# The z1 matmuls of an attention and MLP kernel: operand in shared half-blocks, each row half with its own bank

## The chip, the cores and the metric

The kernel runs on one core of a Trainium2 chip. The metric is the time of one execution in microseconds (us), as the device measures it; it is given as the median of several runs.

## The reference, cut to what matters

One block with two branches that read the same normalised input: attention with 32 heads of 16, and a gated MLP in which z1, one half of the hidden layer, is a plain projection with a gelu.

```python
xn = _layernorm(x, axis=-1)                  # x: 1 x 2048 x 512
z  = _gelu(xn @ w_in)                        # w_in: 512 x 1792
z1 = z[..., :896]
z2 = _layernorm(z[..., 896:], axis=-1)
g  = einsum("ts,bsf->btf", w_sp, z2) + b_sp[None, :, None]   # w_sp: 2048 x 2048
out = x + attention(xn) + (z1 * g) @ w_out
```

All is float32. Where a product needs it, an operand is kept as a high and a low part, and three matmuls stand for one.

## The kernel before, in words

The program is written out instruction by instruction by a planner that runs when the kernel is built. It keeps a clock for each engine (`T`), hands work to TensorE (PE), ScalarE (ACT), VectorE (DVE) and GpSimd (POOL) in that order of time, and so fixes the order of every queue. On the chip only semaphores hold an instruction back; the planner's times are no longer looked at.

Attention sets the beat. PE goes through rounds: eight steps of values (`values`, L1471) in a burst, then eight scores (`scores`, L1363), seven to nine maxima for a later head pair (`maxima`, L1377), and between these the dense slots (`dense_slot`, L1428). The rows of `ORDER` say in which order; two rows alternate, one with nine maxima, one with seven. A dense slot is two matmuls at once, one on PE's upper 64 rows into one bank (`dps[0]`), one on the lower 64 rows into the other. Where PE would have to wait for a PSUM slot and no dense slot may run, the planner puts in a filler (L1442), a slot that multiplies by zero. A dense piece of work that ends more than eight slots into a round stops dense work until the next burst of values ("q", `hold`).

Dense work is a queue of stages: values' projection, q and k (`qk_rest`), `z2_all`, `z1_all`, `spatial` (w_sp times z2), `mlp_out`, `attn_out`.

z1 is computed as 7 blocks f of 128 features by 4 groups g of 512 rows of x, in 14 pairs: for each g the blocks (0, 1), (2, 3), (4, 5), and for odd g block 6 of g - 1 and g together. A pair is 24 slots, one round. The operands are `xnT[g, c]` for the four 128-row parts c of the contraction, and `w1[f]`, each a tile of 128 partitions x 2 parts x 512. Since a matmul has only 64 rows, each part c is split over the two row halves of PE: `both` (L415) first runs the upper half of the contraction of one block and the lower half of the other, then yields "s" and runs the two exchanged, so that each bank is finished by the row half that did not begin it. At an "s" `has_dense` (L1412) puts a `drain` on PE where the last dense slot isn't known to be over.

Transfers are issued by SyncE (SP) with `move`, in the planned order, on one queue. `ahead_of_time` (L356) writes the parts of the z1 weights to the scratch w1scr while the values' projection runs, and `fetch_parts` fetches them from row block NT - 3 of z2 on. `fetch_first` (L603) fetches the four blocks of g = 0 in the last row block of z2; `fetch_xnT` fetches the next group's in the rounds before it is wanted. Each is one DMA of 512 KB over 128 partitions. Tiles come from a ring of 18 (`room["big"]`) and, later, 8 more (`room["old"]`); `place` takes one, `leave` and `lease` give it back, and a "C" task waits until its condition on the rooms holds. `late1` and `kept` are numbers of tiles that weight fetches must leave free.

Names in what follows: dps, the two banks of dense work; wf, fetched weight parts (of w1 or w_sp); zs, the operand of `spatial`, whose pieces are moved by two DMAs of 64 partitions each; qst and kst, the stacked q and k, moved by DMAs of 48 partitions; qst<-mscr, the rows with the running maxima, which the scores need; xt, the operand of z2.

Of the kernel before, what the change touches and what calls it, by code (L numbers as in the profile page):

```python
# [16 lines left out]
P = 128  # L17
S = 2048
D = 512
# [61 lines left out]
LOAD = 5.0  # L81
LOADZ = 6.5
SETTLE = 4.0
HALF = 2.7
SLOT = 0.23
TURN = 0.2
# [6 lines left out]
def fused_block(ctx, tc, x, wqkv, wo, w_in, w_spT, b_sp, w_out, out):  # L93
# [57 lines left out]
    rscr = [[dr.tile([8, 512], F32, name=f"rscr{g}_{c}") for c in range(NG)] for g in range(4)]  # L151
    mscr = [dr.tile([4, 32, 32], F32, name=f"mscr{i}") for i in range(4)]
    wsscr = [dr.tile([P, 2, 512], F32, name=f"wsscr{s}") for s in range(KEPT)]
    w1scr = [dr.tile([P, 2, 512], F32, name=f"w1scr{f}") for f in range(NF)]
    bsplit = dr.tile([2, S], F32, name="bsplit")
    cscr = dr.tile([1, S], F32, name="cscr")
    bscr = [dr.tile([P, D], F32, name=f"bscr{t}") for t in range(NT)]
# [9 lines left out]
    def move(dst, src):  # L167
        nc.sync.dma_start(raw(dst), raw(src))

    def clock():  # L170
        return T["P"]
# [13 lines left out]
    def after(us, fn, *args):  # L185
        at(ends[0] + us, fn, *args)
# [169 lines left out]
    def ahead_of_time(k, a, scr, spare):  # L356

        out = {}
        yield from weight(out, k, a, spare)
        store(scr, out[k])  # L360
        after(2.5, leave, out, k)

    def fetch_parts(out, k, scr, spare):
        yield "C", lambda: clear() and room["big"] + room["old"] > 1 + spare[0]
# [53 lines left out]
        yield "s",  # L418
        yield from dense(n, y, x, (1, 0), False, True, w)

    def need(ok):
        while not ok():
            yield "w", 1.0

    held = [0]
    dfree = [0.0]
# [78 lines left out]
    def v_rest():  # L505

        for t in range(EARLY, NT, 2):
            k = None
            while dfree[0] > clock():
                if sum(f <= clock() for f in slotfree) > 1:  # L510
                    k = take("v", 2)
                    break
                yield "w", 0.05
            if t == VAHEAD:
                for f in range(NF):
                    owed[0] += 1
                    spawn(ahead_of_time(f, (f"w1_{f}", w_in[:, f * P:(f + 1) * P], D, ND), w1scr[f], AHEAD), 1)
                for s in range(KEPT):
                    owed[0] += 1
                    spawn(ahead_of_time(s, sp_weights(0, s), wsscr[s], AHEAD), 1)  # L520

            def ops(t):
                c128 = slice((t % 4) * P, (t % 4 + 1) * P)
                return lambda c: (xnT[t // 4, c][:, 0, c128], xnT[t // 4, c][:, 1, c128], wv[c][:, 0, :], wv[c][:, 1, :])
            for it in both(ND, ops(t), ops(t + 1)):
                if it[0] == "t" and k is not None:
                    it = "t", [[(2 + 2 * k + m[0], *m[1:]) for m in mms] for mms in it[1]]
                yield it
            if t in (2, 6):
# [68 lines left out]
            move(xt[:, :, c * P:(c + 1) * P], xscr[t // 4][c][:, :, (t % 4) * P:(t % 4 + 1) * P])  # L598

    late1 = [5]  # L600
    fetched = [False]

    def fetch_first():  # L603
        for c in range(ND):
            yield "C", lambda: room["big"] + room["old"] > 2
            xnT[0, c] = piece(f"xnT0_{c}_", place(xnT, (0, c)))
            move(xnT[0, c], xscr[0][c])
        fetched[0] = True
        late1[0] = 1

    def z2_all():
        yield from need(lambda: len(w2) == 2 * ND)
        for t in range(NT):
            xt = xts.pop(t)
            if t + 2 < NT:
                yield from need(lambda: room["big"] > 1)
                z2_load(t + 2)
            if t == NT - 6:
                calm[0] = False
            if t == NT - 3:  # L620
                for f in range(NF):
                    spawn(fetch_parts(w1, f, w1scr[f], late1), 1)
            if t == NT - 1:
                spawn(fetch_first(), 1)
            yield from need(lambda: room["big"] > 1)
            z = piece(f"z2_{t}").bitcast(F32).rearrange("p a b -> p (a b)")[:, :FH]
            ops = [lambda c, j=j: (xt[:, 0, c * P:(c + 1) * P], xt[:, 1, c * P:(c + 1) * P], w2[c, j][:, 0, :448], w2[c, j][:, 1, :448]) for j in range(2)]
            yield from both(ND, *ops, 448)
            lease("big", 1)
            yield "e", [z2_out(t, z, j) for j in range(2)]  # L630
            yield "q",
        for k in w2:
            leave(w2, k)

    def z1_out(f, g, bank):
        if bank == 0:
# [36 lines left out]
    kept = [3]  # L673

    def z1_all():
        yield from need(lambda: fetched[0])
        for g in range(NG):
            pairs = [((f, g), (f + 1, g)) for f in (0, 2, 4)]
            if g % 2:
                pairs.insert(0, ((6, g - 1), (6, g)))  # L680
            for n, pair in enumerate(pairs):
                if g == NG - 1 and n == 2:
                    load_b(0)
                    spawn(z_loader(), 2)
                    prepare(wsp, [((0, s), *sp_weights(0, s)) for s in range(KEPT, NT)], spare=kept)
                if (g, n) == FIRST:
                    for s in range(KEPT):
                        spawn(fetch_parts(wsp, (0, s), wsscr[s], kept), 1)
                if n == 2:
                    calm[0] = True  # L690
                if n == (2 if g % 2 else 1) and g + 1 < NG:
                    yield from need(lambda: room["big"] + room["old"] > 4)
                    fetch_xnT(g + 1, 1)
                yield from need(lambda: all(f in w1 for f, _ in pair))
                ops = [lambda c, f=f, h=h: (w1[f][:, 0, c * P:(c + 1) * P], w1[f][:, 1, c * P:(c + 1) * P], xnT[h, c][:, 0, :], xnT[h, c][:, 1, :]) for f, h in pair]
                yield from both(ND, *ops)
                if g == NG - 1:
                    for f in {f for f, _ in pair}:
                        leave(w1, f)
                if g % 2 and n == 0:  # L700
                    drop(g - 1)
                yield "e", [z1_out(f, h, i) for i, (f, h) in enumerate(pair)]
                yield "q",
            if g % 2:
                drop(g)

    def sp_weights(g, s):
        return f"wsp{g}_{s}", w_spT[s * P:(s + 1) * P, g * 512:(g + 1) * 512], 512
# [891 lines left out]
```

## Time and profile before

| | us |
|---|---|
| median of 3 runs | 1824.07 |
| lowest and highest | 1822.53, 1825.53 |
| the profiled execution | 1822.49 |
| its span, first to last instruction | 1820.6 |
| PE busy in the span | 1788.7 |
| DVE busy | 1442.1 |
| ACT busy | 1212.6 |
| POOL busy | 684.7 |

The times of the trace are microseconds from the start of the span. The z1 stage lies from 500 to 686 us of it: its first slot starts at 500.23, its last before the burst of values at 686. A busy share alone says little here: PE is nearly always busy, so it is read by the distance from one slot to the next and by the length of rounds.

### The profile page before, as it was taken

How to read it: one execution, taken by the hardware profiler on the slowest of the kernel's cores; microseconds unless marked ns; L12 is line 12 of the kernel's file. 1: busy time of each engine (PE TensorE's matmuls, PEld its weight loads, DVE VectorE, ACT ScalarE, POOL GpSimd, SP SyncE). 2: the span in 40 equal slices, each digit the busy share in tenths (PEclk: the TensorE clock that was granted, in tenths of full speed). 3: DMA queues.
4: the chain of work that ended last, by engine and by line, in shares of the span. 5: the costliest groups of instructions: out<-in, count | busy, mean ns of one | idle time of the engine just before them, and what ended most of it. 6: DMA issues, size and time to landing. Idle time of an engine off the chain costs nothing.

```text
span 1820.6 us, 38040 instructions
## 1 busy us (share of the span) xinstructions
PE 1788.7 (98%) x14708; PEld 1084.0 (60%) x14708; DVE 1442.1 (79%) x1716; ACT 1212.6 (67%) x1329; POOL 684.7 (38%) x803
## 2 busy tenths in 40 slices
PE   9999999999999999999999999999999999999997
PEld 7666566666566566665656656566565665654542
DVE  8868788888887787787778878878787887887882
ACT  4357777888877776666666656666666665666655
POOL 5442241777788775223622270007121500011201
PEclk9999999999999999999999999999999999999999
DMA  7869854434856356775878597548766766583322
GB/s 264 292 216 306 262 182 127 126 106 130 250 155 204 104 148 168 191 169 165 225 185 185 167 220 167 132 124 226 175 154 165 211 161 144 135 192 99 103 87 82
DMA packets 247261, 314.26 MB, mean 173 GB/s; under 512 B 69072, under 2 KB 139280, under 8 KB 247072
## 3 DMA queue, kind: packets, MB, share of 16 engines
q1 hardware_dynamic: 239592, 284.57, 57.8%
q0 software_dynamic: 7488, 27.27, 4.6%
q8 instruction: 115, 1.88, 0.5%
q14 instruction: 66, 0.54, 0.1%
HBM read 197.45 MB, written 114.30 MB: 171 GB/s over the span
## 4 chain that ended last, share of the span: by engine, by line
PE 93%; DVE 4%; issue 1%; ACT 1%; DMA 0%; POOL 0%; POOLq 0%; DVEq 0%; SPq 0%; ACTq 0%
PE dps L1428 37%; PE sl L1471 25%; PE sl L1363 15%; PE sl L1377 13%; DVE mm L922 4%; ACT pf L110 1%; PE dps L1442 1%; PE sl L276 1%; PE sl L277 1%; PE sl L278 1%; PE sl L1428 0%; PE sl L1169 0%; PE sl L1067 0%; DMA x<-in_x 0%; PE sl L1241 0%
## 5 line engine op out<-in xcount | busy, mean ns | idle before, releaser
L922 DVE TENSOR_REDUCE mm<-sl 128x2 f32<-128x1024 f32 x1008 | 1207.7, 1223 | 176.3 <-PE sl L1377 168.6
L110 ACT ACTIVATE pf<-sl 128x1024 f32<-128x1024 f32 x1024 | 1042.4, 1026 | 347.5 <-PE sl L1363 307.6
L1363 PE MATMUL sl<-qst,kst 50*128 50x512 f32 x2048 | 432.9, 416 | 7.9 <-DVE mm L922 3.0
L1471 PE MATMUL sl<-pf,vhalf 128*32 128x512 f32 x3840 | 438.7, 595 | 0.7 <-DVE on L1057 0.7
L1377 PE MATMUL sl<-kst,qst 48*128 48x512 f32 x2016 | 413.1, 404 | 5.3 <-ACT pf L110 3.2
L1428 PE MATMUL dps<-wsp,zs 64*128 64x512 f32 x2352 | 382.3, 392 | 0.0
L1363 PEld LDWEIGHTS sl<-qst,kst 50*128 50x128 f32 x2048 | 193.5, 184 | 212.3 <-DVE mm L922 76.8
L1471 PEld LDWEIGHTS sl<-pf,vhalf 128*32 128x32 f32 x3840 | 111.6, 109 | 249.4 <-issue 214.1
L1377 PEld LDWEIGHTS sl<-kst,qst 48*128 48x128 f32 x2016 | 191.2, 184 | 112.6 <-ACT pf L110 54.8
L1428 PEld LDWEIGHTS dps<-wsp,zs 64*128 64x128 f32 x2352 | 225.4, 187 | 35.8
L110 ACT ACTIVATE e<-sl 128x512 f32<-128x512 f32 x64 | 38.3, 598 | 183.1 <-PE sl L1471 167.6
L1501 DVE TENSOR_TENSOR e<-sl,e 128x512 f32<-128x512 f32 x64 | 44.3, 692 | 132.5 <-PE sl L1471 74.6
L820 POOL TENSOR_TENSOR hhl<-z1i,hhl 128x512 fp32r<-128x512 f32 x26 | 33.1, 1286 | 278.3 <-ACT hhl L110 278.3
L1428 PE MATMUL dps<-w,xt 64*128 64x448 f32 x768 | 112.4, 368 | 1.7
L1428 PE MATMUL dps<-wout,hp 64*128 64x512 f32 x672 | 110.2, 393 | 0.0
L973 POOL TENSOR_TENSOR ob<-ob 128x512 f32<-128x512 f32 (+1 forms) x16 | 20.5, 1283 | 215.3 <-DMA ob<-rscr 215.3
L1428 PEld LDWEIGHTS dps<-w,xt 64*128 64x128 f32 x768 | 74.8, 186 | 15.1 <-issue 8.1
L1428 PEld LDWEIGHTS dps<-wout,hp 64*128 64x128 f32 x672 | 64.7, 187 | 9.9
L462 POOL TENSOR_TENSOR qkhl<-qr,qkhl 128x512 fp32r<-128x512 f32 x24 | 30.3, 1281 | 89.6 <-ACT qkhl L110 44.6
L969 POOL TENSOR_TENSOR ob<-ob 128x512 f32<-128x512 f32 (+1 forms) x16 | 20.8, 1303 | 107.4 <-DMA ob<-escr 104.1
L1428 PE MATMUL dps<-wf,zs 64*128 64x512 f32 x336 | 55.1, 392 | 0.0
L1428 PE MATMUL dps<-xnT,wqk 64*128 64x512 f32 x288 | 48.1, 394 | 0.3
(286 smaller groups left out, 1725.8 us busy)
## 6 DMA issues: line engine op xcount, KB each, us to landing
zs<-z2scr SPq DMA_DIRECT2D x192, 256.0 KB
escr<-e SPq DMA_DIRECT2D x60, 256.0 KB
hscr<-hhl POOLq DMA_DIRECT2D x28, 512.0 KB, 6.9
qst<-qscr SPq DMA_DIRECT2D x60, 192.0 KB
kst<-kscr SPq DMA_DIRECT2D x60, 192.0 KB
qscr<-qkhl SPq DMA_DIRECT2D x16, 512.0 KB
kscr<-qkhl SPq DMA_DIRECT2D x16, 512.0 KB
xt<-xscr SPq DMA_DIRECT2D x64, 128.0 KB
```

The costliest lines, as they stand in the source:

```text
L110: return nc.scalar.activation(out, in_, func, **kw)
L276: nc.tensor.matmul(acc, lh, rh, start=first, stop=False)
L462: nc.gpsimd.tensor_sub(hl[:, 1, :], raw_, hl[:, 0, :].bitcast(F32))
L820: nc.gpsimd.tensor_sub(hl[:, 1, :], z1, hl[:, 0, :].bitcast(F32))
L922: nc.vector.tensor_reduce(mmax[g][:, :, t, kc], sl[k], AX.X, ALU.max)
L969: nc.gpsimd.tensor_add(both_[rows, 0, :], both_[rows, 0, :], both_[rows, 1, :])
L973: nc.gpsimd.tensor_mul(both_[rows, 0, :], both_[rows, 0, :], both_[rows, 1, :])
L1363: nc.tensor.matmul(sl[k][:, j, :], kst[p % 2][rows, kt * P:(kt + 1) * P], qst[p % 2][rows, c * 512:(c + 1) * 512], start=True, stop=True)
L1377: nc.tensor.matmul(sl[k][:, j, :], qst[p % 2][rows, tt * P:(tt + 1) * P], kst[p % 2][rows, kc * 512:(kc + 1) * 512], start=True, stop=True)
L1428: nc.tensor.matmul(bank_of(bank)[:, :w], lhs, rhs, start=go, stop=stop)
L1471: nc.tensor.matmul(sl[k][cols:cols + VW, 0, :], vpack(p, kt + r, j), pf[:, j * 512:(j + 1) * 512], start=n % CYC == 0, stop=n % CYC == CYC ...
L1501: nc.vector.tensor_add(e, sl[k][:, 0, :], e)
```

## The change

z1's operand becomes eight half-blocks `xp[j]`, j = 0 to 7: half h of part c of the contraction, 64 rows, is stored twice, in the upper and in the lower 64 partitions of one tile. The weights become eight pieces `w1[u, i]`: the upper partitions hold one feature block, the lower the other, for half i of the contraction. With that each row half of PE runs all eight half-blocks of its own block into its own bank, and `both` with its "s" is not used for z1. The tiles xp are filled once for g = 0 and then overwritten in place: after its slots in the pair u = 2, and in the pair u = 3, a half-block asks for the next group's data (`x_next`, `x_half`); the planner holds the slots of a half-block back until LOADX = 6 us after its issue. The stores of w1 are cut in two to match. The tiles of z2's weights are given back one by one in the last round of z2, and not all at its end.

```diff
-    w1scr = [dr.tile([P, 2, 512], F32, name=f"w1scr{f}") for f in range(NF)]
+    w1scr = dr.tile([64, NF, 2, ND, 2, P], F32, name="w1scr")
...
+        if scr is w1scr:
+            for h in range(2):
+                store(scr[:, k, :, :, h, :], out[k][64 * h:64 * h + 64].rearrange("p a (c f) -> p a c f", c=ND), 0.3 + 0.7 * h)
+        else:
+            store(scr, out[k])
+        after(3.0, leave, out, k)
...
+    W1 = ((0, 1), (2, 3), (4, 5), (6, 6))
+    xp, xat = {}, {}
+
+    def x_half(g, j, rows):
+        c, h = divmod(j, 2)
+        for r in rows:
+            move(xp[j][64 * r:64 * r + 64], xscr[g][c][64 * h:64 * h + 64])
+        xat[j] = max(clock(), ends[0]) + LOADX
+
+    def x_next(g, j, rows):
+        xat[j] = FAR
+        later(0.2, x_half, g, j, rows)
+
+    def fetch_w1(u, i, spare):
+        yield "C", lambda: clear() and room["big"] + room["old"] > 1 + spare[0]
+        bulk(2.0)
+        t = piece(f"w1p{u}_{i}", place(w1, (u, i)))
+        for r, f in enumerate(W1[u]):
+            move(t[64 * r:64 * r + 64].rearrange("p a (c h f) -> p a c h f", c=2, h=2), w1scr[:, f, :, 2 * i:2 * i + 2, :, :])
+        yield "T", LOAD
+        w1[u, i] = t
 
     def fetch_first():
-        for c in range(ND):
+        for j in range(2 * ND):
             yield "C", lambda: room["big"] + room["old"] > 2
-            xnT[0, c] = piece(f"xnT0_{c}_", place(xnT, (0, c)))
-            move(xnT[0, c], xscr[0][c])
-        fetched[0] = True
+            xp[j] = piece(f"xp{j}", place(xp, j))
+            x_half(0, j, (0, 1))
         late1[0] = 1
...
-            yield from both(ND, *ops, 448)
+            for n, it in enumerate(both(ND, *ops, 448)):
+                yield it
+                if t == NT - 1 and n > ND:
+                    for j in range(2):
+                        later(0.5, leave, w2, (n - ND - 1, j))
...
-        yield from need(lambda: fetched[0])
         for g in range(NG):
-            pairs = [((f, g), (f + 1, g)) for f in (0, 2, 4)]
+            pairs = [(u, g, g) for u in range(3)]
             if g % 2:
-                pairs.insert(0, ((6, g - 1), (6, g)))
+                pairs.insert(0, (3, g - 1, g))
...
-                if n == (2 if g % 2 else 1) and g + 1 < NG:
-                    yield from need(lambda: room["big"] + room["old"] > 4)
-                    fetch_xnT(g + 1, 1)
-                yield from need(lambda: all(f in w1 for f, _ in pair))
-                ops = [lambda c, f=f, h=h: (w1[f][:, 0, c * P:(c + 1) * P], w1[f][:, 1, c * P:(c + 1) * P], xnT[h, c][:, 0, :], xnT[h, c][:, 1, :]) for f, h in pair]
-                yield from both(ND, *ops)
+                yield from need(lambda: (u, 0) in w1 and (u, 1) in w1)
+                for j in range(2 * ND):
+                    yield from need(lambda: xat.get(j, FAR) <= clock(), 0.1)
+                    c = slice(j % 4 * P, (j % 4 + 1) * P)
+                    ops = lambda _: (w1[u, j // 4][:, 0, c], w1[u, j // 4][:, 1, c], xp[j][:, 0, :], xp[j][:, 1, :])
+                    yield from dense(1, ops, ops, (0, 1), j == 0, j == 2 * ND - 1)
+                    if u == 3:
+                        x_next(g, j, (0,))
+                    elif u == 2 and g == NG - 1:
+                        later(0.7, leave, xp, j)
+                    elif u == 2:
+                        x_next(g + 1, j, (0, 1) if g % 2 else (1,))
```

## Rows read from the trace of the kernel before

**Rows 1.** The page: busy time by engine, and the chain that ended last.
```profile
PE 1788.7 (98%) x14708; PEld 1084.0 (60%) x14708; DVE 1442.1 (79%) x1716; ACT 1212.6 (67%) x1329; POOL 684.7 (38%) x803
...
PE 93%; DVE 4%; issue 1%; ACT 1%; DMA 0%; POOL 0%; POOLq 0%; DVEq 0%; SPq 0%; ACTq 0%
```

**Rows 2.** Busy time by stretch: two rounds of z1, then three single rounds.
```profile
core 0: us, PE busy (x) PEld busy (x) DVE busy (x) ACT busy (x) POOL busy (x), PEclk, DMA share, GB/s
550.20:577.30 27.10, 26.93 (x226) 16.10 (x224) 21.77 (x25) 20.01 (x24) 23.19 (x25) 1.00 0.87 275
...
577.30:591.10 13.80, 13.71 (x118) 8.02 (x116) 10.92 (x11) 10.73 (x13) 9.50 (x10) 1.00 0.23 86
591.10:604.40 13.30, 13.22 (x112) 8.28 (x110) 10.85 (x15) 9.31 (x12) 9.53 (x10) 1.00 0.35 122
```

**Rows 3.** Timeline of PE: start, length, line, tiles; second and last swap of z1.
```profile
517.75 0.40 PE L1377 MATMUL sl<-kst,qst 48*128 48x512 f32 x2
517.98 0.40 PE L1428 MATMUL dps<-xnT__5807,wf 64*128 64x512 f32 x2
518.47 0.50 PE L1428 MATMUL dps<-xnT__5695,wf 64*128 64x512 f32 x2
518.80 0.40 PE L1363 MATMUL sl<-qst,kst 50*128 50x512 f32 x2
...
680.62 0.39 PE L1377 MATMUL sl<-kst,qst 48*128 48x512 f32 x2
680.85 0.39 PE L1428 MATMUL dps<-xnT__7225,wf 64*128 64x512 f32 x2
681.32 0.50 PE L1428 MATMUL dps<-xnT__7120,wf 64*128 64x512 f32 x2
681.66 0.40 PE L1363 MATMUL sl<-qst,kst 50*128 50x512 f32 x2
```

**Rows 4.** Busy time by stretch: two rounds each of the spatial stage.
```profile
712.80:739.40 26.60, 26.60 (x228) 15.98 (x226) 20.86 (x25) 16.85 (x17) 1.28 (x1) 1.00 0.51 120
739.40:766.00 26.60, 26.60 (x228) 16.07 (x226) 21.55 (x25) 17.98 (x19) 9.37 (x9) 1.00 0.84 229
```

**Rows 5.** Fillers: line L1442 from 496 to 690 us, then from 690 to 820.
```profile
nothing on L1442; most used: ['L1428', 'L1471', 'L1363', 'L1377', 'L110', 'L922', 'L168', 'L654', 'L648', 'L656', 'L658', 'L662', 'L664', 'L1501', 'L1413', 'L939', 'L583', 'L564', 'L347', 'L933', 'L934', 'L935', 'L937', 'L585', 'L587']
...
L1442 PE MATMUL dps<-brow,zeror x4: 392/393/393, 725.9 to 779.2; 64*128 64x512 f32 x4
...
779.15 0.40 PE L1442 MATMUL dps<-brow,zeror 64*128 64x512 f32 x2
779.38 0.41 PE L1377 MATMUL sl<-kst,qst 48*128 48x512 f32 x2
779.73 3.64 PE L1471 MATMUL sl<-pf,vhalf 128*32 128x512 f32 x32
```

**Rows 6.** Busy time by stretch, for the last two columns, DMA share and GB/s.
```profile
462.00:483.00 21.00, 20.11 (x172) 13.28 (x172) 18.60 (x25) 17.63 (x21) 16.21 (x22) 1.00 1.05 291
483.00:485.00 2.00, 2.00 (x24) 0.57 (x20) 1.57 (x4) 2.00 (x4) 0.49 (x2) 1.00 0.64 206
485.00:497.50 12.50, 12.15 (x108) 8.36 (x104) 10.93 (x12) 10.30 (x13) 9.69 (x13) 1.00 0.95 317
498.00:501.00 3.00, 3.00 (x29) 1.36 (x22) 2.39 (x6) 2.81 (x5) 1.90 (x5) 1.00 0.00 0
523.00:524.50 1.50, 1.50 (x18) 0.49 (x20) 1.50 (x2) 1.48 (x3) 1.32 (x2) 1.00 1.05 401
534.50:537.00 2.50, 2.50 (x26) 1.67 (x26) 2.32 (x3) 2.21 (x3) 0.91 (x1) 1.00 1.07 179
656.50:659.50 3.00, 3.00 (x30) 2.00 (x30) 2.41 (x3) 2.63 (x4) 0.00 (x1) 1.00 1.04 240
```

**Rows 7.** Timeline of SP's DMA issues: the fetches ahead of z1.
```profile
460.93 0.49 SPq L168 DMA_DIRECT2D wf<-w1scr  x1
...
478.46 0.52 SPq L168 DMA_DIRECT2D wf<-w1scr  x1
...
485.00 0.47 SPq L168 DMA_DIRECT2D xnT__5695<-xscr  x1
...
489.22 0.50 SPq L168 DMA_DIRECT2D xnT__5807<-xscr  x1
489.83 0.52 SPq L168 DMA_DIRECT2D wf<-w1scr  x1
```

**Rows 8.** Timeline of PE: round one of z1, its last part of the contraction.
```profile
508.31 0.43 PE L1428 MATMUL dps<-xnT__5807,wf 64*128 64x512 f32 x2
```

**Rows 9.** Timelines of SP and PE: the maximum rows and the score that needs them.
```profile
596.86 1.27 SPq L168 DMA_DIRECT2D qst<-mscr  x2
...
607.98 0.50 PE L1363 MATMUL sl<-qst,kst 50*128 50x512 f32 x2
```

**Rows 10.** The tile w1scr: its DMA issues, first and last start.
```profile
L168 SPq DMA_DIRECT2D w1scr<-w x7: 320/338/1325, 87.5 to 107.1; - x7
L168 SPq DMA_DIRECT2D wf<-w1scr x7: 327/422/522, 460.9 to 489.8; - x7
```

**Rows 11.** Timelines of POOL and PE: the last conversion of w_sp, its first use.
```profile
701.01 1.29 POOL L349 TENSOR_TENSOR wsp<-wsp_15r,wsp 128x512 fp32r<-128x512 f32 x1
...
704.02 1.09 PE L1428 MATMUL dps<-wsp,zs 64*128 64x512 f32 x8
```

**Rows 12.** Line L1428 from 1649.9 to 1676 us, and L1442 from 1645 to 1680.
```profile
nothing on L1428; most used: ['L1471', 'L1442', 'L1377', 'L1363']
...
L1442 PE MATMUL dps<-brow,zeror x44: 386/397/398, 1654.0 to 1674.7; 64*128 64x512 f32 x44
```

More of the change, by code (lines that the diff above doesn't have):

```diff
@@ L83 @@
 SETTLE = 4.0
+LOADX = 6.0
 HALF = 2.7
@@ L359, in ahead_of_time @@
         yield from weight(out, k, a, spare)
-        store(scr, out[k])
-        after(2.5, leave, out, k)
+        if scr is w1scr:
[4 more added lines that the diff above has]
+        after(3.0, leave, out, k)
     def fetch_parts(out, k, scr, spare):
@@ L419, in both, with need @@
         yield from dense(n, y, x, (1, 0), False, True, w)
-    def need(ok):
+    def need(ok, us=1.0):
         while not ok():
-            yield "w", 1.0
+            yield "w", us
     held = [0]
@@ L516, in v_rest @@
                     owed[0] += 1
-                    spawn(ahead_of_time(f, (f"w1_{f}", w_in[:, f * P:(f + 1) * P], D, ND), w1scr[f], AHEAD), 1)
+                    spawn(ahead_of_time(f, (f"w1_{f}", w_in[:, f * P:(f + 1) * P], D, ND), w1scr, AHEAD), 1)
                 for s in range(KEPT):
@@ L600, in fused_block @@
     late1 = [5]
-    fetched = [False]
+    W1 = ((0, 1), (2, 3), (4, 5), (6, 6))
[16 more added lines that the diff above has]
+        w1[u, i] = t
     def fetch_first():
-        for c in range(ND):
+        for j in range(2 * ND):
             yield "C", lambda: room["big"] + room["old"] > 2
-            xnT[0, c] = piece(f"xnT0_{c}_", place(xnT, (0, c)))
-            move(xnT[0, c], xscr[0][c])
-        fetched[0] = True
+            xp[j] = piece(f"xp{j}", place(xp, j))
+            x_half(0, j, (0, 1))
         late1[0] = 1
@@ L620, in z2_all @@
             if t == NT - 3:
-                for f in range(NF):
-                    spawn(fetch_parts(w1, f, w1scr[f], late1), 1)
+                for u in range(4):
+                    for i in range(2):
+                        spawn(fetch_w1(u, i, late1), 1)
             if t == NT - 1:
@@ L631, in z2_all @@
             yield "q",
-        for k in w2:
-            leave(w2, k)
     def z1_out(f, g, bank):
@@ L675, in z1_all @@
     def z1_all():
-        yield from need(lambda: fetched[0])
         for g in range(NG):
-            pairs = [((f, g), (f + 1, g)) for f in (0, 2, 4)]
+            pairs = [(u, g, g) for u in range(3)]
             if g % 2:
-                pairs.insert(0, ((6, g - 1), (6, g)))
-            for n, pair in enumerate(pairs):
+                pairs.insert(0, (3, g - 1, g))
+            for n, (u, lo, hi) in enumerate(pairs):
                 if g == NG - 1 and n == 2:
@@ L690, in z1_all @@
                     calm[0] = True
-                if n == (2 if g % 2 else 1) and g + 1 < NG:
-                    yield from need(lambda: room["big"] + room["old"] > 4)
-                    fetch_xnT(g + 1, 1)
-                yield from need(lambda: all(f in w1 for f, _ in pair))
-                ops = [lambda c, f=f, h=h: (w1[f][:, 0, c * P:(c + 1) * P], w1[f][:, 1, c * P:(c + 1) * P], xnT[h, c][:, 0, :], xnT[h, c][:, 1, :]) for f, h in pair]
-                yield from both(ND, *ops)
-                if g == NG - 1:
[L698 to L702, printed above, removed]
+                yield from need(lambda: (u, 0) in w1 and (u, 1) in w1)
[10 more added lines that the diff above has]
+                        x_next(g + 1, j, (0, 1) if g % 2 else (1,))
+                if g == NG - 1:
+                    for i in range(2):
+                        leave(w1, (u, i))
+                yield "e", [z1_out(f, h, i) for i, (f, h) in enumerate(zip(W1[u], (lo, hi)))]
                 yield "q",
-            if g % 2:
-                drop(g)
     def sp_weights(g, s):
```

## Prediction

> **What bounds the kernel now.** I read the page first. TensorE (PE) is busy for 98% of the span and holds 93% of the chain of waits; VectorE, second, is at 79% [rows 1]. PE's clock is at its higher level, 2.4 GHz, in every stretch used below (PEclk 1.00) [rows 2]. PE's instructions stand in a fixed order, so the kernel is a row of rounds: eight value steps (L1471), then scores, maxima and 24 dense slots. The busy times of the z1 stage, 496.1 to 699.9 us, show a PE that is never idle for long: two rounds take 27.1 us, of which 26.93 are busy, and DVE, the next engine, has 21.8 [rows 2]. So what is worth something is PE time within a round, and anything that PE itself has to wait for. The timeline of PE at the middle of a z1 pair shows what the change aims at: slots start 0.23 to 0.24 us apart, but at the swap (L1412, a drain) the step is 0.49 and the one after it 0.33 [rows 3]. That is 0.26 + 0.09 = 0.35 us. The same double step is there in all 14 z1 pairs; the last one is shown too [rows 3].
>
> **The drains.** `both` swaps the two banks halfway; the new loop calls `dense` once per half-block with banks (0, 1) throughout and yields no "s", so 14 drains go. Matmuls stay: 24 slots per pair, same sizes, same pitch. Full price: 14 x 0.35 = 4.9 us. But not all of that need come through. The spatial stage has the same rounds without the drain inside, and there two rounds take 26.6 us [rows 4], 0.5 less than 27.1, not 0.7. Its round with nine maxima holds one filler (L1442) just ahead of the last maximum: the planner waited for a PSUM slot and filled the hole [rows 5]. The z1 stage has none [rows 5]; its drain sits where that hole would be. So I take 7 pairs of rounds x 0.5 = 3.5 us, with 2.5 (only the seven rounds with seven maxima gain) and 4.9 as ends.
>
> **The first operand: twice the bytes, in half-height pieces.** Round one of z1 used four blocks xnT of 512 KB and seven w1 pieces, each moved by one DMA over 128 partitions. It will use eight blocks xp, each filled by two DMAs over 64 partitions, and eight w1 pieces, also in two halves. These transfers run in the last z2 rounds, and there the DMA queue has no air: share 1.05 of 16 engines from 462 to 483 us, 0.64 for 2 us, 0.95 from 485 to 497.5, then nothing [rows 6]. Its idle time is 0.36 x 2 + 0.05 x 12.5 = 1.3 us. So whatever is added ends after 497.5.
> What a piece costs depends on its height. 523.0 to 524.5 holds the end of xnT blocks, full height: 401 GB/s. 656.5 to 659.5 holds only the spatial stage's first operands zs, 64 rows, upper and lower in turn, as the new ones: 240 GB/s. 534.5 to 537 holds qst and kst, 48 rows, two DMAs in the same half before the half changes: 179 GB/s [rows 6]. For 0.524 MB that is 1.31, 2.18 and 2.93 us; I take 2.18, the same shape.
> Before, eleven pieces were through at 497.5: w1 from 460.93, the sixth at 478.46, three xnT from 485.00, the fourth at 489.22, the last w1 behind it [rows 7]. Afterwards the eighth xp stands behind six w1 (the spare rule `late1` keeps the others back) and seven xp: 14 pieces x 2.18 - 11 x 1.31 = 30.5 - 14.4 = 16.1 us more, less 1.3 idle: it lands at 497.5 + 14.8 = 512.3. Round one wants its last half-block where its last three slots begin, 508.31 [rows 8], or 508.0 with the drain gone. PE is in order, so it waits 4.3 us, and scores and values queued behind that matmul wait too. The planner doesn't see this: it allows LOADX = 6 us. At 401 GB/s: 18.3 - 14.4 - 1.3 = 2.6, lands at 500.1, no wait. At 179: 41.0 - 14.4 - 1.3 = 25.3, lands at 522.8, a wait of 14.8. That the blocks of w2 come free one by one (before: all after the round) is what lets the last four be issued at all before 495; on PE it costs nothing.
>
> **The reloads.** xp is overwritten in place, each half-block a round ahead of its next use; planned 0.54 us after its slots, so with a round of 13.3 its margin is 12.8 us. At g = 1 to 2 both rows are reloaded, 16 DMAs, 4.19 MB: 17.5 us at 240 GB/s in a round of 13.8 that has 0.23 x 13.8 = 3.2 us of other traffic [rows 2]. It runs over by 6.9 us, inside the margin; at 179 GB/s by 12.8, just at it. Single-row reloads are half of that. The twelve xnT fetches of 512 KB that go (1.31 us each) are in neither sum. On SP's queue each reload first waits for its matmul; behind it stand the running-maximum rows (qst<-mscr), issued by 598.13 and wanted by the score at 607.98 [rows 9]: 9.9 us, which hide an overrun of 6.9. At 179 GB/s they would be 0 to 4 us late; I take 0.
>
> **What I cost at nothing.** w1scr's stores become 14 DMAs with 512-byte runs; the last store is issued at 107.1 and the first fetch at 460.9 [rows 10]: 353 us of cover. The 48 additional x issues take about 0.45 us of SP each (0.39 to 0.50 for xnT [rows 7]), 22 us spread over the stage's 204. Memory blocks: xp holds eight blocks until the last z1 round where xnT held four, so the w_sp rows 8 to 15 are converted later; before, the last ended at 702.30 and row 8 is used from 704.02 on, one row per 1.3 us, so row 15 about 9 us later [rows 11]. If that cover is too short, dense slots slip by up to a round; and that is nearly free, because 1649.9 to 1675.6 are two rounds without any dense work, only fillers [rows 12].
>
> **Sum.** -3.5 + 4.3 = +0.8 us. On the profiled execution 1822.49 us (span 1820.6 and 1.9 around it) that is 1823.3; the median of the three runs, 1824.07, lies 1.6 above that execution, and so I forecast 1824.9. Ends: -4.9 + 0 = 1819.2, and -2.5 + 14.8 = 1836.4.
>
> **Rivals.** *No wait at all*: halves in turn reach both sides of SBUF and a long queue of them runs near 401 GB/s, or the planner issues xp earlier. For it: upper and lower pieces alternate strictly, more regularly than qst and kst. Against: zs alternates as strictly and shows 240 [rows 6]. Time 1824.07 - 3.5 = 1820.6, 1819.2 if the fillers stay away.
> *Half-height at 179 GB/s, slower*: the queue ahead of round one also carries qst, kst and z2 stores, as it did where 179 was seen, and the last half-block lands at 522.8. Price 14.8 us of PE standing still in round one: -3.5 + 14.8 = +11.3, 1835.4. It decides against the change (over 0.2%, 3.65 us) as soon as the pieces run below 220 GB/s: 14 x 2.38 = 33.3 us, landing at 515.1. For it: 179 was measured with the queue full; against: only 48 rows, and in same-half pairs. The Trainium skill (SBUF — State Buffer, "Door 1: The DMA port swizzle") says that partitions 0 to 63 reach half of the 16 ports, 196 GB/s measured, and its section "Can I just issue two DMAs to hit both halves?" says two such DMAs gain only 6%. By that, an estimate of 208 GB/s gives 2.52 us a piece, a landing at 517.1 and 1829.7 us. The trace agrees in direction (240 and 179 against 401) [rows 6], and this is the rule that speaks against the change.
> *A lost round*: w_sp rows come too late, unit boundaries move to rounds with nine maxima; the drains' gain is given back, 1824.
>
> **How the numbers follow.** This kernel's times can be told apart at about 0.2%. Forecast 0.38 (0.05 of it past +0.2%); no wait 0.30 (0.25 of it past -0.2%, since it lies at that bound); half-height slow 0.27; lost round 0.05. Faster 0.25, same 0.43, slower 0.32. The range 1819 to 1834 leaves out the slow rival's upper half and little else; the likeliest case's own range is 1822 to 1828.
>
> **What would show it.** Drains: no 0.49 step inside z1 rounds; two rounds at 26.6, a filler in every second one. Wait: in round one PE idle ahead of a dense slot, released by a DMA, about 4 us, growing over the last half-blocks; DMA share near 1 until about 512. Reloads: no such idle later. I am wrong if round one has no wait, if a later reload has one, or if z1 rounds keep 27.1.

## The result, and the profile after

The changed kernel takes 1831.36 us (median of 6 runs, 1826.46 to 1832.88) against 1823.30 (6 runs) of the kernel before: ratio 1.0038, 95% interval 1.0026 to 1.0051. It is slower by 0.4%. The forecast was 1824.9, which is 0.8 us above the 1824.07 then known and was counted as no change; the kernel lost 8.1 us. The time lies inside the range of 1819 to 1834, but outside 1822 to 1828, the range of the case held likeliest. The profiled execution took 1831.37 us, its span is 1829.3.

In the changed kernel lines below the edit stand 28 further down: dense slots L1456, scores L1391, maxima L1405, values L1499; `move`, above it, is L169. (In the experiments they stand a few lines lower again.) The page still shows PE at 98%, but the chain of waits, in which DMA had 0% [rows 1], now gives it 4%:

```profile
PE 1790.8 (98%) x14708; PEld 1083.9 (59%) x14708; DVE 1443.7 (79%) x1716; ACT 1212.6 (66%) x1329; POOL 685.3 (37%) x803
...
PE 89%; DMA 4%; DVE 4%; ACT 1%; POOL 1%; issue 1%; SPq 0%; POOLq 0%; DVEq 0%; ACTq 0%
```

PE's waits for transfers from 460 to 700 us (line waited for: us in total, times, longest us):

```profile
PE dps L1456 <- DMA xp<-xscr: 7.8, 5, 3.9
PE sl L1391 <- DMA qst<-mscr: 0.7, 1, 0.7
```

I number the rounds from the first burst of values, so that round 29 (496.6 us) is round one of z1 and round 42 its last. Lengths in us, from one burst of values to the next; the last four columns are experiments that come below.

| rounds | before | after | no reload | stacks held | whole weights | both |
|---|---|---|---|---|---|---|
| 27 to 29 | 41.1 | 43.9 | 43.7 | 43.8 | 41.5 | 41.0 |
| 30, 31 | 27.1 | 26.8 | 26.7 | 27.0 | 26.6 | 26.6 |
| 32, 33 | 27.1 | 30.7 | 26.6 | 26.6 | 31.3 | 26.6 |
| 34, 35 | 27.1 | 26.6 | 26.6 | 26.6 | 26.6 | 26.6 |
| 36, 37 | 27.4 | 26.6 | 26.6 | 28.0 | 28.8 | 30.5 |
| 38, 39 | 27.1 | 26.6 | 26.6 | 26.6 | 26.6 | 26.6 |
| 40, 41 | 27.1 | 33.0 | 26.6 | 26.6 | 32.7 | 26.6 |
| 42, 43 | 27.2 | 26.9 | 26.6 | 27.0 | 26.7 | 26.6 |
| sum | 231.2 | 241.2 | 230.2 | 232.2 | 240.7 | 231.2 |

So the stage is 10.0 us longer, and this is the whole of it: ahead of round 27 the profiled execution of after is 0.9 us early, behind round 43 it loses nothing (1120.7 us before, 1120.4 after). Five pairs of rounds gain 2.3 us between them; rounds 27 to 29 lose 2.8, 32 and 33 lose 3.6, 40 and 41 lose 5.9. Busy time by stretch, for the three losing places and one gaining one (the last three columns are granted clock, DMA share, GB/s):

```profile
core 0: us, PE busy (x) PEld busy (x) DVE busy (x) ACT busy (x) POOL busy (x), PEclk, DMA share, GB/s
467.70:482.40 14.70, 13.52 (x114) 8.83 (x112) 12.10 (x17) 11.50 (x15) 8.14 (x13) 1.00 1.07 213
...
538.50:553.30 14.80, 13.63 (x110) 8.15 (x111) 10.54 (x15) 10.38 (x14) 14.10 (x20) 1.00 1.05 192
553.30:569.10 15.80, 14.01 (x115) 8.20 (x114) 11.13 (x11) 9.97 (x12) 10.93 (x12) 1.00 1.03 274
582.10:608.70 26.60, 26.60 (x226) 16.46 (x224) 21.64 (x25) 19.89 (x24) 20.63 (x22) 1.00 0.79 229
649.00:667.30 18.30, 14.39 (x116) 8.42 (x115) 10.99 (x15) 9.42 (x12) 9.53 (x10) 0.87 1.03 223
```

582.1 to 608.7 answers to [rows 4]: 26.60 us, all of it busy, as in the spatial stage. In each losing round the DMA share is over 1 and PE is not busy throughout. (A share over 1 alone does not make a round lose: the last experiment has stretches at 1.03 and 1.04 that lose nothing.) The timeline of PE around the longest wait (in brackets the idle time ahead of a line and what ended it):

```profile
660.53 0.40 PE L1456 MATMUL dps<-xp,w1p 64*128 64x512 f32 x2
664.84 1.22 PE L1456 MATMUL dps<-xp,w1p 64*128 64x512 f32 x4 [3.91 <-DMA xp<-xscr]
...
667.27 4.71 PE L1499 MATMUL sl<-pf,vhalf 128*32 128x512 f32 x32
```

The half-block it waits for is a reload that SP issued at 654.03, behind this queue (start and length of SP's DMA issues):

```profile
645.12 2.06 SPq L169 DMA_DIRECT2D qst<-qscr  x1
647.27 2.23 SPq L169 DMA_DIRECT2D xp<-xscr  x2
649.55 0.57 SPq L169 DMA_DIRECT2D kst<-kscr  x1
650.99 0.45 SPq L169 DMA_DIRECT2D xp<-xscr  x1
651.91 0.31 SPq L169 DMA_DIRECT2D qst<-qscr  x1
652.76 0.34 SPq L169 DMA_DIRECT2D wf<-wsscr  x1
654.03 0.45 SPq L169 DMA_DIRECT2D xp<-xscr  x1
```

Reloads (256 KB each) stand between the loads of the score stacks (qst and kst, 192 KB each). The trace's record of the transfers has the reload of 654.03 complete at 664.8, when PE goes on. The same mixture stands in the queue at 534 to 548 us, ahead of the waits of 1.17 us (till 551.95) and 1.65 us (till 567.28). The reload of both halves (rounds 35 and 36), where no stack load is near, has no wait in this execution.

### The profile page after: what moved, and what is told of

Its sections match the earlier page's. It is cut to its first block, busy times and chain, and to the rows that moved or that the text cites. A ratio compares the mean times of both kernels' runs of the same rounds, so it can differ in the third digit from the quotient of the medians.

```text
span 1829.3 us, 38128 instructions
## 1 busy us (share of the span) xinstructions
PE 1790.8 (98%) x14708; PEld 1083.9 (59%) x14708; DVE 1443.7 (79%) x1716; ACT 1212.6 (66%) x1329; POOL 685.3 (37%) x803
## 4 chain that ended last, share of the span: by engine, by line
PE 89%; DMA 4%; DVE 4%; ACT 1%; POOL 1%; issue 1%; SPq 0%; POOLq 0%; DVEq 0%; ACTq 0%
PE dps L1456 35%; PE sl L1499 24%; PE sl L1391 14%; PE sl L1405 12%; DVE mm L950 3%; DMA xp<-xscr 2%; DMA kst<-kscr 1%; ACT pf L111 1%; PE dps L1470 1%; PE sl L277 1%; PE sl L278 0%; PE sl L279 0%; DMA w1p<-w1scr 0%; PE sl L1456 0%; DVE bst L1175 0%
## 5 line engine op out<-in xcount | busy, mean ns | idle before, releaser
L1391 PE MATMUL sl<-qst,kst 50*128 50x512 f32 x2048 | 433.8, 416 | 8.0 <-DVE mm L950 2.9
L1499 PE MATMUL sl<-pf,vhalf 128*32 128x512 f32 x3840 | 439.8, 597 | 0.9 <-DVE on L1085 0.7
L1405 PE MATMUL sl<-kst,qst 48*128 48x512 f32 x2016 | 416.0, 404 | 5.4 <-ACT pf L111 2.8
L1456 PE MATMUL dps<-wsp,zs 64*128 64x512 f32 x2352 | 382.6, 392 | 0.0
L1391 PEld LDWEIGHTS sl<-qst,kst 50*128 50x128 f32 x2048 | 195.0, 184 | 209.7 <-issue 75.2
L1405 PEld LDWEIGHTS sl<-kst,qst 48*128 48x128 f32 x2016 | 192.3, 185 | 115.7 <-ACT pf L111 53.0
L1499 PEld LDWEIGHTS sl<-pf,vhalf 128*32 128x32 f32 x3840 | 111.7, 110 | 251.4 <-issue 216.2
L1456 PEld LDWEIGHTS dps<-wsp,zs 64*128 64x128 f32 x2352 | 225.8, 187 | 35.6
L1456 PE MATMUL dps<-xp,w1p 64*128 64x512 f32 x672 | 113.2, 397 | 7.8 <-DMA xp<-xscr 7.8
L1456 PE MATMUL dps<-w,xt 64*128 64x448 f32 x768 | 113.0, 368 | 1.7
L1456 PE MATMUL dps<-wout,hp 64*128 64x512 f32 x672 | 110.1, 392 | 0.0
L1456 PEld LDWEIGHTS dps<-w,xt 64*128 64x128 f32 x768 | 75.6, 186 | 15.3 <-issue 8.1
L1456 PEld LDWEIGHTS dps<-xp,w1p 64*128 64x128 f32 x672 | 66.6, 188 | 20.3 <-DMA xp<-xscr 11.0
L1456 PEld LDWEIGHTS dps<-wout,hp 64*128 64x128 f32 x672 | 64.8, 187 | 9.8
```

The source lines that it names most:

```text
L1391: nc.tensor.matmul(sl[k][:, j, :], kst[p % 2][rows, kt * P:(kt + 1) * P], qst[p % 2][rows, c * 512:(c + 1) * 512], start=True, stop=True)
L1405: nc.tensor.matmul(sl[k][:, j, :], qst[p % 2][rows, tt * P:(tt + 1) * P], kst[p % 2][rows, kc * 512:(kc + 1) * 512], start=True, stop=True)
L1456: nc.tensor.matmul(bank_of(bank)[:, :w], lhs, rhs, start=go, stop=stop)
L1499: nc.tensor.matmul(sl[k][cols:cols + VW, 0, :], vpack(p, kt + r, j), pf[:, j * 512:(j + 1) * 512], start=n % CYC == 0, stop=n % CYC == CYC ...
```

## Theories and experiments

Theory M: the loss is the meeting of a reload with the stack loads in one queue, plus the fetches ahead of z1. Rivals: H, the low rate of transfers to 64 partitions is enough by itself, whatever else runs; S, transfers that follow each other into the same 64 partitions are slow by themselves; Q, the bytes and places in the queue count, whatever half they go to; and, for the gain, that the swaps cost nothing. Each ratio below is against runs of the kernel before on the same chip.

**No reload.**

```diff
-        for r in rows:
+        for r in rows if g == 0 else ():
             move(xp[j][64 * r:64 * r + 64], xscr[g][c][64 * h:64 * h + 64])
```

> The changed kernel with every reload of z1's half-blocks for the second to the fourth row group left out: z1 multiplies the first group's operand throughout, so z1 is computed on the wrong rows after its first rounds; no instruction of TensorE is left out. Theory 1 (the loss sits where reloads come late): the waits at 552, 567 and 661 us are gone, rounds 32 and 33 return from 14.85 and 15.84 to 12.95 and 13.66 us and rounds 40 and 41 from 18.28 and 14.71 to the same, 9.5 us in all, so 1831.4 - 9.5 = 1821.9 us. Theory 2 (only the idle time shown as waits belongs to reloads, 1.17 + 1.65 + 3.91 = 6.7 us): 1824.7 us. Theory 3 (the rounds are long for a cause other than the reloads, the stack loads or the order of SP's queue): 1830 to 1832 us. All: the rounds 27 to 29 ahead of the first reload stay as they are, 2.8 us longer than before.

z1 keeps the first group's operand throughout. 1820.53 us, ratio 0.9983 (0.9975 to 0.9992). Rounds 32, 33, 40 and 41 are back at 26.6 a pair; rounds 27 to 29 stay at 43.7. So the late losses are the reloads, and what remains without them is a gain: rounds 30 to 43 take 186.4 us, before 190.1, 3.6 less.

```profile
540.20:553.10 12.90, 12.90 (x110) 7.87 (x110) 10.55 (x15) 10.21 (x14) 12.21 (x19) 1.00 0.54 119
...
646.70:659.60 12.90, 12.90 (x112) 8.02 (x111) 10.56 (x15) 9.18 (x12) 9.55 (x10) 1.00 0.83 222
```

Those are the busy times of rounds 32 and 40: DMA share 0.54 and 0.83 without the reload, over 1 with it.

**The swaps put back, without reloads.** To the edit of "no reload" comes this one.

```diff
                 for j in range(2 * ND):
+                    if j == ND:
+                        yield "s",
```

> a_no_reload with the swap of row halves put back in the middle of each of z1's 14 block pairs (the step of 0.49 and 0.33 us of the kernel before); as in a_no_reload z1 keeps the first row group's operand. Theory D (each swap costs the 0.26 us by which a pair of rounds is shorter without it; 14 swaps, 3.5 us, bounds 2.5 to 4.9): 1820.5 + 3.5 = 1824.0 us, rounds of 13.3 and 13.8 us in z1. Rival (z1's rounds are set by other engines, and the swaps only show there): 1820.5 us, under 1 us apart.

1824.80 us, ratio 1.0006 (0.9998 to 1.0015), 0.0023 or 4.2 us above the kernel without swaps; rounds 30 to 43 take 190.0 us against 186.4. The swaps are worth 3.6 us there, and the steps of 0.49 and 0.33 of [rows 3] are back as 0.50 and 0.34 (548.42 to 548.92 and 549.26; the second slot is folded into the first line), in the timeline of PE:

```profile
548.19 0.41 PE L1407 MATMUL sl<-kst,qst 48*128 48x512 f32 x2
548.42 1.00 PE L1458 MATMUL dps<-xp,w1p 64*128 64x512 f32 x4
549.26 0.41 PE L1393 MATMUL sl<-qst,kst 50*128 50x512 f32 x2
```

**Reload whole.** A half-block comes as one transfer of 128 partitions and 512 KB; the reloads are those of rounds 31, 35 and 38, and the operand is then not the one that z1 needs.

```diff
+        if g and rows != (0,):
+            move(xp[j], xscr[g][c])
-        for r in rows:
+        for r in rows if g == 0 else ():
```

> The changed kernel, but a half-block is reloaded whole, 128 partitions and 512 KB in one transfer, at the same place in the order where now one row half of it is loaded or both are, and not at all in the rounds of the left-over block, so that every group's reload costs the same 512 KB a half-block as now in sum. What lies in the operand is then not what z1 needs, so z1 is wrong. Theory H (transfers to 64 partitions of one half are slow, whatever their sum): the loads run at over 300 GB/s, the waits at 552 and 567 us vanish or fall under 0.5 us each, and the one at 661 us too: 1821 to 1824 us. Theory B (the number of bytes that come in z1 is the cause): each reload of 4 MB stands in one round in place of two, so waits are as long or longer: 1831 to 1836 us.

1827.61 us, ratio 1.0022 (1.0013 to 1.0030): between the two. Round 32, where 4 MB now meet the stack loads, takes 20.2 us and round 33 15.0; PE's waits there:

```profile
PE dps L1458 <- DMA xp<-xscr: 5.1, 3, 2.5
```

The reloads of rounds 35 and 38 meet no stack loads, or only as they end, and cost nothing (rounds 36 to 41 at 12.9 to 13.7 us). Full height does not save a reload that meets them. Whether half height harms one that doesn't is not so clear: behind the half-height reload of both halves, round 36 takes 13.0 us in the changed kernel, but 14.1 to 16.1 in each of the six experiments below that keep it. Neither theory had this outcome.

**Halves in turn.**

```diff
         for r in rows:
+            r = r if len(rows) == 2 or j % 2 == 0 else 1 - r
```

> The changed kernel, but where one row half of each of the eight half-blocks is reloaded (rounds 31, 32, 38 and 39), the half alternates from one half-block to the next, upper and lower in turn; number, size and order of the transfers stay, and the operand that z1 finds is the wrong one in half of them. Theory S (transfers that follow each other into the same 64 partitions are slow, those in turn are not, as in rounds 35 and 36 where they ran at some 280 GB/s without a wait): the waits in rounds 32, 33 and 40 fall by more than half, 1823 to 1826 us. Theory Q (it is the bytes and transfers ahead in the queue while the stack loads run, whatever half they go to): 1830 to 1833 us, waits as before.

Half of the operand is then the wrong one. 1831.64 us, ratio 1.0046 (1.0034 to 1.0058), as the changed kernel. S falls as the cause: which half a transfer goes to makes no difference to the time, and the two rounds lose as before. The rate does depend on it. While the reload of round 38 is nearly alone in the queue, it moves 198 GB/s into one half in the changed kernel (first line) and 228 in turn here (second line); then the busy times of rounds 32 and 40 of this experiment:

```profile
634.00:640.00 6.00, 6.00 (x56) 2.57 (x54) 3.37 (x5) 4.11 (x6) 4.06 (x5) 1.00 1.02 198
...
634.00:640.00 6.00, 6.00 (x54) 2.67 (x52) 3.46 (x4) 4.60 (x6) 2.90 (x4) 1.00 1.04 228
...
538.20:552.50 14.30, 13.28 (x112) 8.01 (x110) 10.58 (x15) 10.22 (x14) 13.60 (x20) 1.00 1.05 212
...
650.20:667.50 17.30, 13.47 (x116) 8.02 (x117) 10.63 (x15) 9.45 (x12) 9.53 (x10) 1.00 1.04 220
```

**Stack loads late.** Within z1 they wait for the 24th of a head pair's 64 scores (the expectation says "until z1 is done", which is not quite what the edit does). `busy1` is true from the start of z1 to that of the spatial stage.

```diff
-             if p + 1 < NP and stacks[0] <= p and i >= (3 if p else 20) and (i >= LATE or calm[0] and not owed[0]):
+             if p + 1 < NP and stacks[0] <= p and i >= (3 if p else 20) and (i >= LATE or calm[0] and not owed[0] and not busy1[0]):
```

> The changed kernel, but the loads of the score stacks (48 rows each) that fall among z1's rounds wait until z1 is done; nothing is left out. Theory M (waits arise where the reload of one row half meets these loads): rounds 32, 33, 40 and 41 fall to 12.95 and 13.66 us and the time to 1822, provided the stacks are not missed later on. Theory H alone (the low rate of reloads to one half is enough): rounds 32, 33 keep at least 2 of their 3.6 us and round 40 at least 3 of its 5.9: 1827 to 1830 us. If the stack loads are missed afterwards, rounds ahead of the score products grow behind z1 and the time is 1826 to 1835 us with z1's rounds short.

1822.30 us, ratio 0.9994 (0.9985 to 1.0002). Rounds 32, 33, 40 and 41 are at 26.6 a pair, with every reload in place, half height and same half. For these four rounds H alone falls with that, and M holds. Round 36, behind the reload of both halves, now takes 14.7 us.

**Stack loads held while a reload runs.**

```diff
+    def reloading():
+        return any(v > clock() for v in xat.values())
...
-             if p + 1 < NP and stacks[0] <= p and i >= (3 if p else 20) and (i >= LATE or calm[0] and not owed[0]):
+             if p + 1 < NP and stacks[0] <= p and i >= (3 if p else 20) and (i >= LATE or calm[0] and not owed[0] and not reloading()):
```

> The changed kernel, but no stack load is issued among z1's rounds while a reload of a half-block is under way; between the reloads they go as soon as they do now; nothing is left out. Theory M (a reload and the stack loads may each run in z1, only not together): rounds 32, 33, 36, 40 and 41 all at 12.95 to 13.7 us, 1820.5 us as without reloads (1819.5 to 1822.5). If the stacks' own lateness costs score products: 1823 to 1828 us, with waits of score products for stack loads in rounds 33 to 42.

1823.20 us, ratio 0.9999 (0.9990 to 1.0007). The four rounds are again undisturbed; the stacks are issued at 563 to 574 and 653 to 662 and no score waits for one from round 30 on. 1.4 us go in round 36, 1.7 with the late loads, which I had not expected. M and Q are not told apart: holding the eight stack loads also takes 1.5 MB each time out of the queue of these rounds, and no run puts other loads in their place.

**The kernel before with late stack loads.** The same edit as under "stack loads late", in the kernel before.

> The kernel before, with the stack loads among z1's rounds put off until z1 is done, as in c_stacks_late; nothing is left out. If putting them off does nothing by itself: 1823.5 us, within 1 us of the kernel before, and what c_stacks_late gains over the changed kernel is the meeting with the reloads. If the kernel before was held up by these loads too: 1820 to 1822 us.

1823.49 us, ratio 0.9999 (0.9990 to 1.0008). Putting the loads off gains nothing by itself.

**Weights in two whole transfers, short runs.**

```diff
-    w1scr = dr.tile([64, NF, 2, ND, 2, P], F32, name="w1scr")
+    w1scr = dr.tile([P, 4, 2, 2, 2, 2, P], F32, name="w1scr")
...
-        for r, f in enumerate(W1[u]):
-            move(t[64 * r:64 * r + 64].rearrange("p a (c h f) -> p a c h f", c=2, h=2), w1scr[:, f, :, 2 * i:2 * i + 2, :, :])
+        for h in range(2):
+            move(t.rearrange("p a (c h f) -> p (a c) h f", c=2, h=2)[:, :, h], w1scr[:, u, i, h].rearrange("p a c f -> p (a c) f"))
```

> The changed kernel, but the weights of z1 lie in DRAM so that each of the eight pieces is fetched by two transfers of 128 partitions (before: two of 64 each to one half); the stores ahead of it are 32 in place of 14, with the same bytes but for block 6 written twice; nothing is left out. If the rounds 27 to 29 are 2.8 us longer because the fetches of weights and first half-blocks run at the rate of 64 partitions: the waits at 508 and 510 us vanish and the time is 1831.4 - 2.8 = 1828.6 us, half of that if only the weights gain by it. If the number of bytes sets them: 1831 us, no change. If the added stores stand in the way of others in the attention stage: over 1832 us, with the rounds there longer.

1841.05 us, ratio 1.0096 (1.0083 to 1.0109): a miss. Rounds 27 to 29 take 49.5 us; in them a maximum waits 2.3 us for kst and a score 2.3 us for the maximum rows. Round 3, where the weights are stored, is 2.0 us longer. Whether the runs of 512 bytes or the many stores do it this run does not tell.

**Weights in one whole transfer, long runs.**

```diff
+    w1scr = dr.tile([P, 4, 2, ND, 2, P], F32, name="w1scr")
...
-        for r, f in enumerate(W1[u]):
-            move(t[64 * r:64 * r + 64].rearrange("p a (c h f) -> p a c h f", c=2, h=2), w1scr[:, f, :, 2 * i:2 * i + 2, :, :])
+        move(t.rearrange("p a (c h f) -> p a c h f", c=2, h=2), w1scr[:, u, :, 2 * i:2 * i + 2])
```

> The changed kernel, but each weight piece is fetched by one transfer of 128 partitions with runs of 2 KB (in d_w1_whole two transfers with runs of 512 bytes, now two of 64 partitions with runs of 2 KB); the stores ahead are 16 in place of 14, as large as now; nothing is left out. If half-height fetches of the weights cost the front of z1: rounds 27 to 29 fall from 43.9 to 41.5 to 42.5 us, 1829 to 1830 us. If bytes and room set it, no change: 1831 us. If d_w1_whole was slow because of what a transfer to 128 partitions does to the rest rather than its short runs, it is slower again: over 1834 us.

Rounds 27 to 29 take 41.5 us in place of 43.9, so the loss ahead of z1 goes with the fetch of the weights in halves. Its size is not firm: the seven kernels that fetch them in the changed kernel's way show 41.8 to 44.6 us there, one execution each. Busy times of rounds 27 and 29:

```profile
467.70:481.50 13.80, 13.28 (x118) 8.43 (x119) 12.06 (x17) 11.52 (x15) 8.09 (x13) 1.00 1.08 236
...
495.10:509.10 14.00, 13.56 (x114) 8.30 (x112) 11.86 (x17) 11.28 (x14) 8.49 (x14) 1.00 1.05 273
```

But the time is 1830.29 us, ratio 1.0038 (1.0025 to 1.0051), which is the ratio of the changed kernel: 2 us go again in rounds 36 and 37.

**Both halves in one transfer, with and without the hold.** The weights come as in "weights in one whole transfer", and a half-block for both halves is brought by one transfer that reads its 64 rows twice. A reload of one half stays a transfer to 64 partitions.

```diff
-        for r in rows:
+        if len(rows) == 2:
+            move(xp[j].rearrange("p a f -> p (a f)"), xscr[g][c][64 * h:64 * h + 64].rearrange("(o p) a f -> o p (a f)", o=1).to_broadcast([2, 64, 1024]))
+        for r in rows if len(rows) == 1 else ():
```

> The changed kernel with three things of the transfers altered and nothing left out: the stack loads held while a reload runs (as in i_hold), each weight piece fetched by one transfer of 128 partitions (as in k_w1_one), and a half-block that goes to both row halves brought by one transfer to 128 partitions that reads its 64 rows twice (now two transfers to 64 partitions). If the loss is the time that the transfers take and no more: rounds 27 to 29 at 41.2 us as before, rounds 32, 33, 36, 40 and 41 undisturbed, so 1823.6 - 3.7 for the swaps = 1819.9 us (1818.5 to 1821). If reading the same rows twice is no faster than two transfers of half height: round 36 keeps 1 to 2 us, 1821 to 1822 us.

> As n_all, but the stack loads go where they go in the changed kernel; nothing is left out. Theory M: rounds 27 to 29 and 36 as in n_all, but rounds 32, 33, 40 and 41, where a reload of one row half (still 64 partitions) meets the stack loads, keep their 9 us: 1828 to 1830 us. If half-height transfers elsewhere held the queue up for these rounds too: 1820 to 1825 us.

1951.89 us with the hold (ratio 1.0708), 1961.86 without (1.0765): far off both expectations. While these transfers run, the DMA engines are busy for 0.13 of their time, two of sixteen, and move 52 GB/s; PE waits 93.6 us for xp with the hold and 98.9 without.

```profile
510.00:515.00 5.00, 0.00 (x0) 0.00 (x0) 0.00 (x0) 0.00 (x0) 0.00 (x0) 0.50 0.13 52
```

The Trainium skill (DMA: Bandwidth & Descriptors, section "Rules for kernel authors") says that an outermost dimension of c copies with stride zero confines a DMA to at most c engines. The trace agrees: c is 2 here, and 0.13 of 16 engines is 2.1.

**Hold and whole weights together.** The edits of "stack loads held" and "weights in one whole transfer".

> The changed kernel with the stack loads held while a reload runs (i_hold) and each weight piece fetched by one transfer of 128 partitions (k_w1_one); half-blocks come in two transfers of 64 partitions as in the changed kernel; nothing is left out. If the two losses add up and no third one stands behind them: rounds 27 to 29 at 41.4 us (43.8 in i_hold), rounds 32, 33, 40 and 41 undisturbed, round 36 at 14 to 15 us as in i_hold and k_w1_one, so 1823.2 - 2.4 = 1820.8 us, 0.14% under the kernel before (0.05 to 0.25%). If holding the stacks only moved the loss: 1823 us or more.

1821.75 us, ratio 0.9988 (0.9979 to 0.9997): 0.12% under the kernel before, just clear of the noise. Its interval overlaps that of the hold alone (0.9990 to 1.0007), so what the weights add to the time is not shown. Rounds 27 to 29, 32 and 33, 40 and 41 are all repaired:

```profile
469.40:510.40 41.00, 39.95 (x338) 24.86 (x336) 35.88 (x49) 34.39 (x42) 29.97 (x45) 1.00 1.04 278
537.10:563.70 26.60, 26.60 (x230) 15.95 (x228) 21.64 (x25) 20.53 (x25) 23.83 (x30) 1.00 0.95 253
590.30:606.40 16.10, 15.23 (x116) 8.71 (x116) 11.03 (x15) 9.70 (x12) 9.53 (x11) 0.94 0.90 212
647.40:674.00 26.60, 26.60 (x228) 15.91 (x227) 21.67 (x25) 19.93 (x24) 19.04 (x20) 1.00 1.03 237
```

The third line is round 36, the one loss left: 3.1 us in this execution, which is the slowest of the 11.

## Why the prediction was right or wrong

**The sum, term by term.** Forecast were -3.5 us for the drains, +4.3 for the first operand and 0 for the reloads. The profiles show -3.6, +2.8 and +10.5, which makes 9.7 of the 10.0 us by which the stage is longer. That 1831.36 lies in the range is luck: the range reached so high for a longer wait in round one, which did not come, and the time went where the prediction had put nothing.

**The drains: right in size, wrong in one detail.** Forecast 3.5 us (2.5 to 4.9); the rounds with and without swaps differ by 3.6, the rounds before and after without reloads by 3.6. The pair of rounds came to 26.6 as forecast. No filler stands in z1, though: the round with nine maxima takes 13.66 us without one (13.78 with the swap), the one with seven 12.95 (13.30). [rows 5] did not bear on it.

**The first operand: landing right, place of the loss wrong.** 240 GB/s and a landing of the last half-block at 512.3 were forecast; the last six half-height pieces of xp end 1.04 us apart (252 GB/s) and the last is complete at 510.3. The loss is 2.8 us against 4.3 forecast, but only about 1.1 of it is the wait in round one that I described, and "halves in turn", the same up to there, has no such wait in its one trace. Another 1.4 is in rounds 27 and 28: the score stacks and the maximum rows stand in the same queue behind the weights, and scores come later (the wait of 0.7 us for qst<-mscr). I had followed the pieces of the new operands through the queue, not those of others behind them. With whole weight fetches 2.4 of the 2.8 us are gone, in executions whose scatter there is as large.

**The reloads: the step that failed.** "Single-row reloads are half of that" and "I take 0" cost 10.5 us: rounds 32 and 33 take 30.7 us where they take 26.6 without reloads, rounds 40 and 41 33.0. The overrun was worked out for the reload of both halves, with the other traffic of the round at 577.3 us, a share of 0.23 [rows 2]. The single reloads lie in other rounds. The kernel before shows what stands there, rounds 32 and 40:

```profile
536.90:550.20 13.30, 13.22 (x112) 8.16 (x110) 10.82 (x15) 10.28 (x14) 11.99 (x18) 1.00 0.38 102
645.60:658.90 13.30, 13.22 (x116) 8.16 (x116) 10.90 (x15) 9.32 (x12) 9.52 (x10) 1.00 0.54 142
```

A single reload is 2.1 MB, 8.7 us at 240 GB/s or 0.66 of a round; with 0.38 and 0.54 that is 1.04 and 1.20. The rows would have said that the queue is full in just these two rounds. Two terms were worse still. The price of 240 GB/s was for halves in turn, and a single reload goes into one half, at 198. And the change moved other loads: without reloads these rounds have shares of 0.54 and 0.83 (under "no reload"), not 0.38 and 0.54.

Even so, a full queue need not make PE wait, and by the prediction's margin of 12.8 us none of these overruns would have. The margin failed too. It counts from an issue 0.54 us after the slots. The last slot of this half-block in round 39 starts at 648.17, SP issues the reload at 654.03, PE wants it at 660.93 (664.84 less the wait of 3.91), and it is complete at 664.8. Nearly 6 us were gone before the transfer was issued, and it took 10.8 more. The first line is from the timeline of PE, the second from SP's own waits between 640 and 662 us:

```profile
648.17 0.39 PE L1456 MATMUL dps<-xp,w1p 64*128 64x512 f32 x2
...
SPq L169 <- DMA xp<-xscr: 5.8, 6, 1.4
```

SP waits there for its own earlier transfers. In the trace's record each issue around 654 us comes right behind the end of the eighth transfer before it (654.03 behind 653.97), so what stands in a slow queue is also issued late. The double reload, which I had looked at as the heavy one, had no wait in the changed kernel; its last transfer was issued at 600.23 and complete 6.7 us later. The prediction named a wait for a later reload among the things that would make it wrong ("if a later reload has one"), and no rival held it; the 0.32 for slower stood on round one alone.

**A second price.** After 3.9 us without a matmul the granted clock is at 0.50 of its higher level, that is 1.2 GHz, in the stretch that follows:

```profile
664.80:669.00 4.20, 4.16 (x22) 1.91 (x26) 1.82 (x2) 1.99 (x4) 1.32 (x2) 0.50 0.76 240
```

The next burst of values takes 4.71 us where others take 3.64, which is 1.1 us. Rounds 40 and 41 are 6.4 us longer than without reloads, and the wait is 3.9 of it; I put most of the other 2.5 down to the clock, an estimate that no run here tests.

**The rivals.** *No wait at all* is out. *Half-height at 179 GB/s* had the sign and nearly the time (1835.4), but not the mechanism: in round one the pieces ran at 252 GB/s and PE waited 1.1 us, not 14.8. The Trainium skill's rule (SBUF — State Buffer, "Can I just issue two DMAs to hit both halves?"), from which the prediction made an estimate of 208 GB/s, is not borne out in that size: halves in turn end 0.89 us apart in the double reload of the changed kernel (296 GB/s) and 1.06 to 1.13 us apart in six variants (233 to 246), whole half-blocks of 512 KB 1.26 us apart (416). Its direction holds: in turn is a little better than one half (228 against 198 GB/s) and far from whole. *A lost round* did not come: from round 44 on the rounds are as before.

**Left open.** Why the same double reload ended 0.89 us apart in the changed kernel and 1.06 to 1.13 us apart in the variants, which then lose 1.2 to 3.1 us in round 36, no run tells: neither the halves (in turn in all of them) nor the stack loads (held or late in three) explain it. The experiments ran on several chips, and each has one profiled execution.

## What to carry to other kernels

Add a transfer to the traffic of the very round in which it runs, read as DMA share of that stretch. Where the sum passes 1, the queue falls behind; that is a warning and no more, since the last kernel has a share of 1.03 in rounds 40 and 41 and no score there waits for a load. So ask next which transfer comes last, when it gets into the queue, and whether an in-order engine wants it before it can be there. A small bulk load next to another one can cost more than a large one by itself, so look at what stands between the pieces in the queue. Holding one class of loads while the other runs was enough here to take away the loss of 0.4%; with the weights fetched in one piece of full height as well, the kernel is 0.1% faster than before.

## What the runs showed of the hardware that I had not expected

A transfer that reads 64 rows twice for 128 partitions runs on two of the sixteen DMA engines, at 52 GB/s, where one over 128 different rows moves 416. A queue of transfers to alternating halves moved more than one to a single half (228 against 198 GB/s), but was no better in its effect on the waits (1831.64 against 1831.36 us). And SP's queue had eight transfers under way at most around 654 us of the changed kernel, so a reload asked for at 648 was issued at 654.
